# Chunk-select attention with a gated convolution: constants made on chip, bounds for fewer queries, gate sums over both halves

## The chip, the cores and the metric

The kernel runs on one core of a Trainium2 chip. The metric is the device time of one execution in microseconds, the median of several runs. Engines are named as in the profile: PE is TensorE, DVE VectorE, ACT ScalarE, POOL GpSimd, SP SyncE; PEld is TensorE's weight load.

## The reference

The input is q, k and v of 4 batches, 8 heads, 768 positions and 64 channels. Keys are cut into 24 chunks of 32. Each query sees the six chunks with the highest upper bound of its score, of those that are not in its future, and within them only positions up to its own. The attention output, with the heads side by side as 512 channels, goes through a gated unit: a causal convolution of five taps per channel gives the gate, a matrix gives the value, and a second matrix the output.

```python
ub = np.sum(np.maximum(q[:, :, :, None, :] * k_min[:, :, None, :, :],
                       q[:, :, :, None, :] * k_max[:, :, None, :, :]), axis=-1)
causal = pos[:, None] // chunk >= np.arange(nc)[None, :]
ub = np.where(causal, ub, -1000000000.0)
top_chunks = np.argsort(ub, axis=-1)[..., -top_k:]
scores = scale * np.matmul(q, k.transpose(0, 1, 3, 2))
mask = sel & (pos[:, None] >= pos[None, :])
attn = softmax of the masked scores
x = np.matmul(attn, v), heads side by side
gate_pre += conv_w[k][None, None, :] * xp[:, k:k + S, :]     # k = 0..4, xp padded in front
gate = 1.0 / (1.0 + np.exp(-gate_pre))
out = (gate * (x @ w_val)) @ w_out
```

A query below 192 has at most six chunks that are not in its future, so that all of them are among its six.

## The kernel before

Work goes by pairs of heads: 16 pairs, four to a batch. A pair's two heads fill 128 partitions. Every operation is recorded with an engine, a key and a cost (`Plan.add`); `Plan.order` then lists all operations by start times that it reckons from these costs, and picks among those that could start at nearly the same time the one with the smallest key. The table `SHIFT` moves the keys of groups of operations. The instructions are issued in that order, and every engine works its own off in order. PSUM's eight banks are given out by the same planner: `CAPS` says how many banks each kind of tile may hold (`w` is all that is not scores, value sums or spare). In places where TensorE would be idle, the planner puts dummy matmuls on `junk` into a spare bank (L530).

For each pair:

- `load` (L447) brings keys, queries and values, with two DMAs for each, one per head. Three buffers each.
- `kq`: TensorE transposes keys and queries (L548). ACT copies the keys out of PSUM to `k32` (L559), the queries to `q32` (L581), and their positive part to `rq` (L586). DVE takes the maximum and the minimum of each chunk (L565). GpSimd casts keys to `KE` (L573), queries to `QU` (L592) and values to `VA` (L636). `KE` also holds, in rows of its own, a -240 for each position's chunk, the E rows. From the extremes comes the table `KB` (L607, L614).
- `sel`/`part`: the bounds of a tile of 128 queries are two fp32 matmuls with `rq` and `q32` as weights and `KB` moving (L664), for the query tiles 1 to 5 (`SELT` is 5); tile 0 needs no selection. DVE adds a table of penalties for future chunks, `cfill`, into `t_mub` (L671), finds the eight highest (MAX8, L680), and compares with the sixth: `NS` is 1 where a chunk isn't chosen (L687). TensorE transposes `NS` (L697). For pairs 0 and 1 ACT and DVE copy the result straight into `QU`'s mask rows (L720). From pair 2 on (`MDMA = 2`) ACT copies it to `t_m` (L711), and two DMAs take it to `QU` (L715).
- `attn`: scores (L793) with `KE` as weights, into 11 banks of up to 512 columns; the E rows times the mask rows make the penalty. Exp on ACT (L800), the diagonal cut by GpSimd (L807), value sums (L824) with the exps as weights. A column of ones in `VA` gives the sum; DVE takes its reciprocal (L750) and multiplies (L754) into `t_onat`. A transposing DMA puts that into `xT` (L766); for the last pair TensorE and ACT do it (L775, L780).
- `moe_gate`: one channel tile per pair. The convolution runs over the two halves of 384 positions. The first `PTAPS` taps are matmuls with diagonal matrices, two for each tap since a weight is split into a high and a low part (L850); the other taps are added by DVE in PSUM (L859). `PTAPS` is 1, but 3 and 5 for the last two tiles of the last batch. ACT takes the tanh (L863).
- `moe_val` and `moe_out`, once a batch is complete: 32 value matmuls (L874), the product with the gate on DVE (L881), 24 output matmuls (L890), a copy (ACT L896, DVE L900) and a store (L903).

At the start, `constants` loads the identity, the E rows and `cfill` by DMA, fills other constants on DVE and GpSimd, and `warm` puts dummy matmuls (L507, L530) in front of TensorE's first transposes. `moe_diag` makes the 20 diagonal matrices on DVE (L931).

Of the kernel before, what the change touches and what calls it, by code (L numbers as in the profile page):

```python
# [9 lines left out]
FP = mybir.dt.float32  # L10
# [6 lines left out]
class Op:  # L17
    __slots__ = ("eng", "key", "cost", "fn", "kind", "reads", "writes", "new", "need", "ndep",
                 "outs", "after", "ready", "end", "num", "at")


class Plan:
# [18 lines left out]
    def add(self, eng, key, cost, fn, r=(), w=(), new=(), kind=None, at=0.0):  # L41
# [6 lines left out]
        key = round(key + self.shift.get(eng + ":" + what, 0.0), 4)  # L48
        o.eng, o.key, o.cost, o.fn, o.kind, o.new, o.at = eng, key, cost, fn, kind, new, at
        o.reads, o.writes = tuple(r), tuple(w)  # L50
# [33 lines left out]
    def order(self, bufs, caps, filler):  # L84
# [9 lines left out]
        for o in self.ops:  # L94
            tags.update(o.new)
            for x in set(o.reads + o.writes + tuple(n for n, _ in o.new)):
                users.setdefault(x, []).append(o)
        engs = ("PE", "ACT", "DVE", "POOL", "SP", "ACTQ")
        free = dict.fromkeys(engs, 0.0)
        wait = {e: [o for o in self.ops if o.eng == e and o.ndep == 0] for e in engs}  # L100
        last_pe = {n: [u for u in users[n] if u.eng == "PE"][-1] for n in tags
                   if tags[n] in caps and n in users}
# [14 lines left out]
        def clear(o, name):  # L117

            mine = set(users[name])
            for u in users[name]:  # L120
                for d in list(u.need) + [self.maker[x] for x in u.reads if x in self.maker]:
                    if d not in mine and d.end is None:
                        return False
                if u is not o and u.new and slot(u) is None:
                    return False
            return True

        def bank_of(tag):

            same, best = [], None  # L130
            for i, n in enumerate(banks):
                t = 0.0 if n is None else over(n)
                if n is not None and tags[n] == tag:
                    same.append(t)
                if t is not None and (best is None or t < best[0]):
                    best = (t, i)
            if best is None:
                return None
            lim = 0.0
            if len(same) >= caps[tag]:  # L140
                known = sorted(x for x in same if x is not None)
                k = len(same) - caps[tag]
                if len(known) <= k:
                    return None
                lim = known[k]
            return max(best[0], lim), best[1]

        def slot(o):
            t = 0.0
            for name, tag in o.new:  # L150
                if tag in caps:
                    got = bank_of(tag)
                    if got is None or tag == "w" and not clear(o, name):
                        return None
                    t = max(t, got[0])
                    continue
# [22 lines left out]
        def matmul(o, s):  # L179

            n = o.cost
            ld = max(pe["ldw"], pe["mm"])
            if o.kind == "u":
                m = max(s, ld + 0.043)
                ld = max(ld + 0.111, m)
                m = max(m + 0.043, ld + 0.043)
                pe["ldw"], free["PE"] = ld + 0.111, m + 0.043
            elif o.kind == "t":
                m = max(s, ld + 0.043)
                pe["ldw"], free["PE"] = ld + 0.108, m + n / 1200 + 0.001  # L190
            else:
                m = max(s, ld + 0.03)
                pe["ldw"], free["PE"] = ld + 0.028, m + n / 2400 + 0.002
            pe["mm"] = m
            if o.kind not in ("t", "x"):
                work.append((m, 0.13 if o.kind == "u" else n / 2400))
            pe["kind"] = "long" if o.kind is None and n >= 250 else o.kind
            o.end = m + (398 + n) / 2400 + 0.05
# [44 lines left out]
        while left:  # L243
# [6 lines left out]
            if e == "PE" and busy(s) < 0.42 and (s > free[e] + 0.12 or o.kind or o.cost < 250):  # L250
# [3 lines left out]
            for name, tag in o.new:  # L254
                if tag in caps:
                    i = bank_of(tag)[1]
# [7 lines left out]
                else:  # L264
# [31 lines left out]
def kernel(  # L296
# [10 lines left out]
    nc = tc.nc  # L307
# [17 lines left out]
    CC = (1, 0)  # L325
    SELT = NT - 1
    NBUF = 3

# [4 lines left out]
    MDMA = 2  # L333
    KBPOOL = True

    PTAPS = {(b, ct): 1 for b in range(B) for ct in range(NCT)}
    PTAPS[B - 1, NCT - 2] = 3
    PTAPS[B - 1, NCT - 1] = 5
    DTAPS = [max(PTAPS[b, ct] for b in range(B)) for ct in range(NCT)]

    ident_np = np.eye(128, dtype=np.float32)
    e_np = np.zeros((64, S), dtype=np.float16)
    for c in range(NCH):
        e_np[c, c * CH:(c + 1) * CH] = PEN
    cfill_np = np.zeros((128, SELT, 2, NCH), dtype=np.float32)
    for it in range(1, NT):
        for p in range(128):
            cfill_np[p, it - 1, :, (it * 128 + p) // CH + 1:] = -1.0e9
    cfill_np = cfill_np.reshape(128, SELT * 2 * NCH)

    ident_dr = nc.inline_tensor(ident_np, name="identc")
    e_dr = nc.inline_tensor(e_np, name="echunk")
    cfill_dr = nc.inline_tensor(cfill_np, name="cfill")
# [3 lines left out]
        "SP:kn": -0.2, "ACTQ:kn": -3.6, "SP:qn": 0.7, "ACTQ:E00": -0.6, "SP:vn": -0.62,  # L357
        "SP:cwn": -4.1, "DVE:KB": -1.2, "POOL:NS": 4.8, "POOL:VA": 1.2, "DVE:diag1": 3.8,
        "DVE:diag": 3.6, "PE:knT": -1.9, "ACT:k32": -2.0, "DVE:kmx": 1.8, "DVE:kmn": 1.6,
        "POOL:KE": -0.8, "DVE:KBh": 2.8, "PE:qnT": -1.88, "ACT:q32": -0.4, "ACT:rq": -0.2,  # L360
        "POOL:QU": -7.4, "DVE:top8": -2.0, "DVE:NS": -4.0, "PE:sT": -0.6, "POOL:kmrr": -1.2,
        "POOL:KBh": -4.6, "PE:s": 0.36, "bank0": 0.67, "ACT:P": 0.15, "POOL:Ptri": 0.3,
        "PE:av": -1.2, "bank1": 0.53, "DVE:rcp": -2.5, "DVE:onat": -1.8, "bank3": -0.2,
        "bank4": -0.06, "bank5": -0.04, "bank6": -0.55, "bank7": 0.1, "bank8": 0.12,
        "bank9": -0.62, "bank10": -0.24, "PE:pg": 1.23, "ACT:m16": -4.6, "PE:pv": 0.4,
        "DVE:gv": -3.4, "PE:po": 0.35, "ACT:osb": 1.5, "PE:xTp": 0.9,
    }
    CAPS = {"w": 5, "s": 4, "av": 2, "spare": 2}
    BUFS = {"kn": 3, "qn": 3, "vn": 3, "P5": 2, "kmx": 2, "kmr": 2,
            "q32": 2, "k32": 2, "rq": 2, "mub": 2, "top8": 2, "onat": 2, "rcp": 2, "osb": 4, "m16": 2}  # L370
# [13 lines left out]
    cfill = cpool.tile([128, SELT * 2 * NCH], FP, tag="cfill")  # L384
# [15 lines left out]
    PB = [ps.tile([128, 512], FP, tag=f"bank{i}", name=f"bank{i}") for i in range(Plan.NBANK)]  # L400
# [38 lines left out]
    def load(p, which, key, engs=("SP", "SP"), halves=((0, 1),)):  # L439
        b, h0 = p // NCT, 2 * (p % NCT)  # L440
        src = dict(kn=k, qn=q, vn=v)[which]
        for n, ws in enumerate(halves):
            t0, t1 = 3 * ws[0], 3 * ws[-1] + 3
            for hh in range(2):
# [12 lines left out]
    def constants():  # L457
        dve(-9, 0.2, lambda: nc.vector.memset(junk, 0.0), w=("junk",))
        sp(-9, 64, lambda: nc.scalar.dma_start(out=ident, in_=ident_dr.ap()), w=("ident",),
           eng="ACTQ")  # L460
        load(0, "kn", -8.9, ("SP", "ACTQ"), ((0,), (1,)))
        load(0, "qn", -8.88, ("SP", "ACTQ"), ((0,), (1,)))
        sp(-8.7, 96, lambda: nc.scalar.dma_start(out=KE[0][HP[1], 0, :], in_=e_dr.ap()),
           w=("E00",), eng="ACTQ")
        sp(-8.6, 120, lambda: nc.scalar.dma_start(out=cfill, in_=cfill_dr.ap()), w=("cfill",),
           eng="ACTQ")
# [3 lines left out]
        sp(-8.2, 10, lambda: nc.sync.dma_start(  # L470
            out=cwn, in_=moe_conv_w.rearrange("k (c p) -> (k c) p", p=128)), w=("cwn",))
        load(1, "vn", -8.1)
        for i in range(2):
            dve(-8.8, 0.15, lambda i=i: nc.vector.memset(KB[i], 0.0), w=(("KB", i),))
        for i in range(NBUF):
            dve(-8.7 + i, 0.5, lambda i=i: nc.vector.memset(QU[i][HP[1], 0, :], 0.0),
                w=(("QM", i, 0, 0), ("QM", i, 0, 1)))
            dve(-8.7 + i, 0.5, lambda i=i: nc.vector.memset(QU[i][HP[0], 1, :], 0.0),
                w=(("QM", i, 1, 0), ("QM", i, 1, 1)))
        dve(-8, 0.2, lambda: nc.vector.tensor_copy(out=identh, in_=ident), r=("ident",),  # L480
            w=("identh",))
        for i in range(NBUF):
            for hh in range(2):
                if i or hh:
                    pool(-4 + 1.5 * i, 0.87, lambda i=i, hh=hh: nc.gpsimd.tensor_copy(
                        out=KE[i][HP[1 - hh], hh, :], in_=KE[0][HP[1], 0, :]),
                        r=("E00",), w=(f"E{i}{hh}",))
        for i in range(2):
            pool(-7.5 + i, 0.6, lambda i=i: nc.gpsimd.memset(NS[i], 0.0),
# [4 lines left out]
        dve(-6, 0.1, lambda: nc.vector.memset(xT[:, :, 0:XP], 0.0),  # L494
# [3 lines left out]
    def warm():  # L498
        pe(-10, 512, lambda: spare("warm", 0, 512, True), r=("junk",), w=("warmed",),
           new=new("warm", "spare", [128, 512]))  # L500
        pe(-9.9, 6 * 512, warm_rows, r=("junk", "warm"), w=("warmed2",),
           new=new("warm2", "spare", [128, 512]))

    def warm_rows():

        def half(r, name, n, st=True):
            nc.tensor.matmul(out=T[name][:, 0:n], lhsT=junk[r, n % 128:n % 128 + 128],  # L507
                             rhs=junk[r, 0:n], start=st, stop=True, skip_group_check=True)

        lo, hi = slice(0, 64), slice(64, 128)  # L510
        for _ in range(4):
            half(lo, "warm", 512)
            half(hi, "warm2", 512)
        for _ in range(2):
            spare("warm", 0, 512, True)
        for _ in range(6):
            half(lo, "warm", 128)
            half(hi, "warm2", 128)
        for _ in range(3):
            spare("warm", 0, 128, True)  # L520
            half(lo, "warm", 128)
            half(hi, "warm2", 128)
        for _ in range(3):
# [488 lines left out]
```

## Time and profile before

| What | Value |
|---|---|
| Median of 3 runs | 201.23 us (200.47 to 202.47) |
| Profiled execution, its own time | 204.38 us |
| Its span, first to last instruction | 202.7 us |
| PE busy | 192.2 us (95%), 2140 matmuls |
| DVE busy | 167.8 us (83%) |
| ACT busy | 158.9 us (78%) |
| POOL busy | 127.8 us (63%) |
| DMA | 30.73 MB, mean 152 GB/s |

The page gives busy time per engine, and the span in 40 slices of about 5 us. Busy time is a union: two instructions that overlap count once, so that the mean duration of one is often more than the distance from one to the next. The chain of waits is followed back from the last instruction, and says at each step what released it. `PEclk` is the TensorE clock that was granted.

### The profile page before, as it was taken

To read this page: it belongs to the slowest core of one execution; us is meant where nothing else is said; L and a number is where in the kernel's file an instruction comes from. 1 tells how busy PE (TensorE), PEld (TensorE's weight loads), DVE (VectorE), ACT (ScalarE), POOL (GpSimd) and SP (SyncE) were. 2 spreads that over 40 slices of the span, in tenths; PEclk is the share of its full clock that TensorE was granted. 3 is DMA by queue.
4 is the path that set the end of the run, shared out by engine and by line. 5 is a ranking of instruction groups with operands and counts; after the bars stand their busy time and mean duration, and the time that the engine had idled before them with its cause. 6 is when DMAs were issued, how large, how long until landed. Compare 5 with 4: busy or idle time off the path is not lost.

```text
span 202.7 us, 6045 instructions
## 1 busy us (share of the span) xinstructions
PE 192.2 (95%) x2140; PEld 153.7 (76%) x2140; DVE 167.8 (83%) x518; ACT 158.9 (78%) x346; POOL 127.8 (63%) x282
## 2 busy tenths in 40 slices
PE   7998489999999999999999999999999999999992
PEld 1556469999986799979897899787989776665550
DVE  5059861977999899999998999999999999988251
ACT  0214368799899999899999999899998989995321
POOL 6647364898978979768867786589676872230000
PEclk9999757999999999999999999999999999999999
DMA  6999994799979699799889687223424112135044
GB/s 140 233 217 218 198 225 73 160 167 212 207 155 176 137 215 204 153 214 192 188 219 225 181 209 175 47 40 98 141 83 128 67 39 54 63 85 207 5 155 155
DMA packets 93277, 30.73 MB, mean 152 GB/s; under 512 B 88138, under 2 KB 90174, under 8 KB 93246
## 3 DMA queue, kind: packets, MB, share of 16 engines
q1 hardware_dynamic: 90222, 28.60, 64.7%
q0 software_dynamic: 1056, 1.05, 3.5%
q10 hardware_dynamic: 1968, 0.68, 1.5%
q8 instruction: 17, 0.28, 0.6%
q14 instruction: 14, 0.11, 0.2%
HBM read 21.27 MB, written 6.29 MB: 136 GB/s over the span
## 4 chain that ended last, share of the span: by engine, by line
PE 85%; ACT 7%; DVE 2%; DMA 2%; issue 1%; POOL 1%; ACTq 0%
PE bank L793 17%; PE bank L664 13%; PE bank L890 10%; PE bank L874 10%; PE bank L548 10%; PE bank L824 10%; PE bank L850 7%; PE bank L530 4%; ACT t_P L800 4%; PE bank L507 2%; PE bank L697 2%; DMA t_vn<-in_v_dram 2%; DVE diag L931 2%; ACT t_k L559 1%; POOL KE L573 1%
## 5 line engine op out<-in xcount | busy, mean ns | idle before, releaser
L800 ACT ACTIVATE t_P<-bank 128x512 f16<-128x512 f32 (+1 forms) x176 | 92.8, 614 | 2.1 <-PE bank L793 1.6
L859 DVE SCALAR_TENSOR_TENSOR bank<-xT,cwT,bank 128x384 f32<-128x384 f16 x116 | 70.9, 616 | 4.3 <-PE bank L850 3.4
L793 PE MATMUL bank<-QU,KE 128*128 128x128 f16 (+4 forms) x448 | 63.4, 252 | 1.3 <-ACT t_P L800 0.8
L592 POOL CAST QU<-t_q 64x384 f16<-64x384 f32 x64 | 32.0, 504 | 24.3 <-PE bank L793 15.6
L793 PEld LDWEIGHTS <-KE 88*128 88x128 f16 (+1 forms) x448 | 37.6, 107 | 8.0 <-issue 1.2
L807 POOL TENSOR_SCALAR_AFFINE_SELECT t_P<-t_P 128x384 f16<-128x384 f16 x64 | 32.9, 524 | 15.0 <-ACT t_P L800 13.2
L573 POOL CAST KE<-t_k 64x384 f16<-64x384 f32 x64 | 32.4, 514 | 8.7 <-ACT t_k L559 5.4
L824 PEld LDWEIGHTS <-t_P 128*128 128x128 f16 x672 | 29.9, 99 | 6.3 <-ACT t_P L800 2.3
L824 PE MATMUL bank<-VA,t_P 128*128 128x65 f16 x672 | 33.9, 193 | 0.4 <-ACT t_P L800 0.4
L664 PEld LDWEIGHTS bank<-KB,t_rq 128*128 128x128 f32 x160 | 27.5, 194 | 2.3 <-ACT t_q L581 0.9
L874 PE MATMUL bank<-xT,wval_sb 128*128 128x384 f16 x128 | 29.0, 326 | 0.0
L890 PE MATMUL bank<-wout_sb,t_gv 128*128 128x512 f16 x96 | 28.4, 379 | 0.0
L664 PE MATMUL bank<-KB,t_rq 128*128 128x48 f32 (+1 forms) x160 | 27.6, 254 | 0.5 <-ACT t_q L581 0.5
L664 PEld LDWEIGHTS bank<-KB,t_q 128*128 128x128 f32 x160 | 27.6, 193 | 0.4
L664 PE MATMUL bank<-KB,t_q 128*128 128x48 f32 (+1 forms) x160 | 27.0, 251 | 0.0
L565 DVE TENSOR_REDUCE t_kmr<-t_k 128x12 f32<-128x384 f32 x32 | 17.4, 545 | 7.7 <-ACT t_k L559 7.7
L559 ACT ACTIVATE t_k<-bank 128x384 f32<-128x384 f32 x32 | 16.5, 516 | 8.1 <-PE bank L548 7.7
L581 ACT ACTIVATE t_q<-bank 128x384 f32<-128x384 f32 x32 | 16.4, 516 | 7.9 <-PE bank L548 7.5
L850 PE MATMUL bank<-xT,diag 128*128 128x384 f16 x88 | 22.3, 326 | 0.0
L863 ACT ACTIVATE t_g<-bank 128x384 f32<-128x384 f32 x32 | 16.5, 518 | 5.0 <-DVE bank L859 2.9
L881 DVE SCALAR_TENSOR_TENSOR t_gv<-t_g,bank 128x384 f16<-128x384 f32 x32 | 17.6, 549 | 2.8 <-PE bank L874 2.4
L896 ACT ACTIVATE t_osb<-bank 128x512 f32<-128x512 f32 x22 | 13.0, 624 | 6.4 <-PE bank L890 5.4
(55 smaller groups left out, 277.6 us busy)
## 6 DMA issues: line engine op xcount, KB each, us to landing
t_vn<-in_v_dram SPq DMA_DIRECT2D x32, 192.0 KB
out_dram<-t_osb SPq DMA_DIRECT2D x24, 256.0 KB
t_kn<-in_k_dram SPq DMA_DIRECT2D x30, 192.0 KB
t_qn<-in_q_dram SPq DMA_DIRECT2D x30, 192.0 KB
QU<-t_m SPq DMA_DIRECT2D x28, 30.0 KB
wval_sb<-in_moe_w_val_dram POOLq DMA_DIRECT2D x1, 512.0 KB, 8.6
wout_sb<-in_moe_w_out_dram POOLq DMA_DIRECT2D x1, 512.0 KB, 7.9
xT<-t_onat SPq DMA_TRANSPOSE x15
```

The source lines that it names most:

```text
L548: lambda tl=tl: nc.tensor.transpose(out=T[name][:, tl * 128:(tl + 1) * 128], in_=T[which, p][:, 3 * w + tl, :], identity=ident),
L573: pool(k0 + (0.6 if p else 2.5), 0.56, lambda hh=hh: nc.gpsimd.tensor_copy(out=ke[HP[hh], hh, sl], in_=T["k32", p][HP[hh], sl]), r=(("k32" ...
L592: pool(k0 + 0.3, 0.56, lambda hh=hh: nc.gpsimd.tensor_copy(out=qu[HP[hh], hh, sl], in_=T["q32", p][HP[hh], sl]), r=(("q32", p, w), ("q32", ...
L664: pe(key, 48, lambda it=it, ts=ts, j=j, x=x: nc.tensor.matmul(out=cols(T[pu][:, it - 1 - i0, :]), lhsT=T[x, p][:, ts], rhs=cols(kb[:, j, : ...
L793: pe(kk, m, lambda hh=hh, c=c, jt=jt, q0=q0, m=m, bank=bank: nc.tensor.matmul(out=T[bank][:, c:c + m], lhsT=ke[KP[hh], hh, jt * 128:(jt + ...
L800: nc.scalar.activation(out=T[pt][:, 0:width], in_=T[bank][:, 0:width], func=AF.Exp, scale=0.125),
L807: nc.gpsimd.affine_select(out=ap, in_=ap, pattern=[[0, tris], [1, 128]], compare_op=ALU.is_ge, fill=0.0, base=0, channel_multiplier=-1)
L824: nc.tensor.matmul(out=T[pav][:, o0:o0 + D + 1], lhsT=T[pt][:, col:col + 128], rhs=va[:, hh, jt, :], start=st, stop=sp_, skip_group_check= ...
L850: nc.tensor.matmul(out=T[pg], lhsT=diag[ct][:, ki, hl, :], rhs=xT[:, slot, X0 + w * HB + ki:X0 + w * HB + ki + HB], start=(n == 0), stop=( ...
L859: dve(kk, 0.525, lambda pg=pg, i=i, c0=c0: nc.vector.scalar_tensor_tensor(out=T[pg], in0=xT[:, slot, c0:c0 + HB], scalar=cwT[:, i:i + 1], ...
L874: pe(key, HB, lambda ct=ct: nc.tensor.matmul(out=T[pv], lhsT=wval_sb[:, ct, et * 128:(et + 1) * 128], rhs=xT[:, slot0 + ct, XP + w * HB:XP ...
L890: pe(key, DM, lambda et=et: nc.tensor.matmul(out=T[po], lhsT=T["gv", b, et][:, s * 128:(s + 1) * 128], rhs=wout_sb[:, et, :], start=(et == ...
```

## The change

In `part`, bounds, comparison and mask now begin at query 192 (`SEL0`). Of tile 1 only the upper 64 queries are computed: their matmuls have 64 weights columns, and the transposed mask has 576 columns for 640. The penalty is added in PSUM, in place, and only for the four chunks of a tile's own 128 positions; MAX8 and the comparison read PSUM. The mask copies of all pairs go straight from PSUM to `QU` (`MDMA = 99`), one on DVE and one on ACT, and the 28 DMAs are gone.

In `moe_gate`, for the first three batches one DVE instruction adds a tap for both halves, over two banks, and one tanh takes both. All `PTAPS` are 1, so that in the last batch DVE adds four taps of each half where TensorE did up to five; 8 diagonal matrices are left of 20.

In `moe_val`, the last batch's value matmuls of the first three channel tiles have earlier keys, and hold a bank of a kind of their own (`v`, up to four) until the fourth.

In `constants`, the identity, the E rows and the penalties are made by GpSimd with fills and selects, the copies of the E rows and two fills move to DVE, and a dummy exp loads ACT's table. Pair 0's keys are loaded first; its casts to `KE` and `QU` are made by ACT from PSUM. `warm` keeps eight short dummies, one per bank, and one of 512 columns; the planner adds five more ahead of the first transposes. Loads are made three pairs ahead. There is one spare bank for two. The planner now gives out several banks at once, reckons with half the clock before 7 us, has other limits for dummies, and every number in `SHIFT` is another.

Some branches of the new code are not taken (`SHUF = 99`, `KDIR`, `RQP`, `UTAPS` all 0).

The core of the diff:

```diff
+    SEL0 = 192
-    MDMA = 2
+    MDMA = 99
     PTAPS = {(b, ct): 1 for b in range(B) for ct in range(NCT)}
-    PTAPS[B - 1, NCT - 2] = 3
-    PTAPS[B - 1, NCT - 1] = 5
+    WIDE = {(b, ct) for b in range(B - 1) for ct in range(NCT)}
-    CAPS = {"w": 5, "s": 4, "av": 2, "spare": 2}
+    CAPS = {"w": 5, "s": 4, "av": 2, "spare": 1, "v": 4}
...
+        def identity():
+            nc.gpsimd.memset(ident, 0.0)
+            select(ident, [[-1, 128]], ALU.not_equal, 1.0, 0, 1)
+
+        def chunk_rows():
+            t = KE[0][HP[1], 0, :]
+            nc.gpsimd.memset(t, PEN)
+            select(t, [[1, S]], ALU.is_ge, 0.0, 0, -CH)
+            select(t, [[-1, S]], ALU.is_ge, 0.0, CH - 1, CH)
...
             for hh in range(2):
+                if p == 0:
+                    act(k0 + 0.3, 0.4, lambda hh=hh: nc.scalar.copy(
+                        out=ke[HP[hh], hh, sl], in_=T[name][HP[hh], :]),
+                        r=rd, w=(("KE", iN, hh, w),))
+                    continue
...
         for it in its:
-            ts = slice(it * 128, (it + 1) * 128)
+            ts = slice((it + 1) * 128 - rows(it), (it + 1) * 128)
             for j, x in enumerate(("rq", "q32")):
-                    out=cols(T[pu][:, it - 1 - i0, :]), lhsT=T[x, p][:, ts],
+                    out=cols(bound(it - 1 - i0))[0:rows(it)], lhsT=T[x, p][:, ts],
...
-            out=cols(T["mub", p][:, i0:i1]), in0=cols(T[pu]), in1=cols(cf[:, i0:i1]),
-            op=ALU.add),
+            out=own(), in0=own(), in1=cfill[:, i0:i1], op=ALU.add),
...
-                    in_=T["mub", p][:, it - 1, s * NCH:s * NCH + m]),
+                    in_=bound(it - 1 - i0)[:, s * NCH:s * NCH + m]),
...
+            for ki in range(max(taps, 1), late):
+                dve(kk, 0.525 if not whole else 0.93, lambda i=i, ki=ki, w=w:
+                    nc.vector.scalar_tensor_tensor(
+                        out=both() if whole else T[pgs[w]], in0=x_of(X0 + ki, w),
+                        scalar=cwT[:, i:i + 1], in1=both() if whole else T[pgs[w]],
+                        op0=ALU.mult, op1=ALU.add),
...
-            pe(key, HB, lambda ct=ct: nc.tensor.matmul(
+            pe(key if early is None or ct == NCT - 1 else early, HB,
+               lambda ct=ct: nc.tensor.matmul(
...
-        if p + 2 < NPAIR:
-            for which in ("kn", "qn", "vn"):
-                load(p + 2, which, p - 0.5)
+        if p + 3 < NPAIR:
+            for n, which in enumerate(("kn", "qn", "vn")):
+                load(p + 3, which, p + 0.1 * n, ENGS)
```

## The prediction

> **What bounds the kernel now.** I read the page first (busy shares, the 40 slices, the chain of waits), then a table of three stages cut at the times at which the slices change, then the chain in order of time, then the start and the tail instruction by instruction.
>
> ```profile
> PE   7998489999999999999999999999999999999992
> DVE  5059861977999899999998999999999999988251
> PEclk9999757999999999999999999999999999999999
> PE 85%; ACT 7%; DVE 2%; DMA 2%; issue 1%; POOL 1%; ACTq 0%
> ...
> core 0: us, PE busy (x) PEld busy (x) DVE busy (x) ACT busy (x) POOL busy (x), PEclk, DMA share, GB/s
> 0.00:40.00 40.00, 34.63 (x267) 24.34 (x268) 23.73 (x90) 17.10 (x37) 24.09 (x53) 0.87 1.02 186
> 40.00:167.00 127.00, 125.94 (x1600) 110.25 (x1600) 120.82 (x383) 120.43 (x266) 99.59 (x222) 1.00 0.72 155
> 167.00:203.00 36.00, 31.66 (x278) 19.11 (x275) 23.30 (x47) 21.41 (x44) 4.14 (x8) 1.00 0.30 102
> ```
>
> The chain is TensorE for 85%. A busy PE isn't a full one, so I priced its work by the pieces of the chain: L664 (bounds) x10 1.05 us, that is 0.108 each; L548 x6 0.66; L824 x23 0.71; L850 x6 0.98; L874 x6 0.97; L890 x12 2.59; the scores L793 of one pair are 5376 columns, 2.3 us at the pace of the others. Times their counts: bounds 34.6, transposes L548 21.3, scores 36, value sums L824 20.8, gates L850 14.3, L874 20.7, L890 20.7, mask transposes L697 4.4: 172.7 us of real work. In the first 40 us only some 15 us of it is done (49 of 192 transposes, 48 of 320 bounds, 28 scores, 42 value sums). The other 158 us fill the 159 us from 40 to the last matmul at 198.8. So from 40 us on TensorE is the bound and full, with DVE and ACT at 95% beside it, and the first 40 us lose 25 us. Two things can pay: an earlier start, and less TensorE work.
>
> The start, from the timeline and the chain:
>
> ```profile
> 5.10 1.28 ACT L559 ACT_TABLE_LOAD   x1 [5.10 <-DMA t_kn<-in_k_dram]
> 7.57 2.98 PE L530 MATMUL bank<-junk 128*128 128x512 f16 x13
> 10.39 0.38 PE L548 MATMUL bank<-ident,t_kn 128*128 128x128 f32 x2
> ...
> 18.73 3.16 DVE diag L931 x11
> ...
> 23.50 0.40 PE L697 MATMUL bank<-identh,NS 128*128 128x128 f16 x2 [2.59 <-DVE NS L687]
> 26.36 1.09 ACT L800 ACTIVATE t_P<-bank 128x512 f16<-128x512 f32 x2 [1.13 <-PE bank L793]
> ```
>
> The keys have been there since 5 to 6 us (what waited for them went on at 5.10), but the first transposes stand behind a fixed run of dummy matmuls until 10.4. Then DVE makes 20 diagonals, 11 of them on the chain ahead of the selection; TensorE runs dry at 21 to 23.5, and its clock is halved in three slices. The first exp is at 26.4, the masks of pair 1 at 40.06.
>
> [...] here the clock fell to 0.50 at 23 us after two idle microseconds or so, and back at 33. [...] 384 elements took 548 ns from PSUM (L754) and 545 from SBUF (L565). [...]
>
> **The change, part by part.**
>
> Start. Constants come from GpSimd, the SP and ACT queues issue keys of pair 0, keys of pair 1, queries of pair 0 first, and the first transposes stand behind 8 + 6 dummies. *Identity*: on GpSimd it stands behind a 64x768 fill (0.75, from NS 128x640 at 0.65), two selects of that size (1.0 each, from 0.52 for 384), and small ones (1.1): 0.8 + 3.9 gives 4.7, [...]. The dummies end at about 4.6 and cost nothing. *Key transposes*: 5.5 to 6.7. *ACT*: seven copies at its pace of 0.39, 6.2 to 9; then eight for the queries (the loads before them are about 1.2 MB at some 215 GB/s, there by 8), 12.1, three more key copies, 13.3. *DVE*: its memsets and five E copies end at about 8; minima and maxima follow the second key copy at 8.5, five at 0.46, then the bound table (1.3 in the trace, and 0.3): 12. *Selection*: bounds 0.8, DVE 0.9, transposes and mask copies 0.9, scores 0.5: first exp at 15.5, against 26.4. The diagonals, now 8 instead of 20, stand behind it. Gain 11 us. Bounds: [...] if TensorE also stays warm at 12 to 20, where it was cold at 23 to 33, up to 15. After that the plan does the same work up to the masks of pair 1, ACT about 0.4 per copy, so I carry the 11 us on unchanged.
>
> Bounds and mask transposes. The tile of queries 128 to 255 is computed for 64 queries: 32 of 160 bound matmuls, two records each, 0.054 saved per record by the halved load: 3.45 us. 16 of 80 mask transposes move 64 columns instead of 128: 0.027 each, 0.4. All of this is on the bound engine: -3.85. If the load weren't shortened, 0 instead of 3.45.
>
> DVE in the middle, per pair, at the pace of back-to-back instructions. Gate adds: eight at 0.585 (3.50 us for six in the tail) become four of 768 elements; [...] 0.985 each: 4.7 to 3.9. Penalty and its tile: 0.33 to 0.2. Mask copy: new, 0.40 to 0.45 (24x640 took 489, 24x384 355). MAX8 from PSUM: ten, [...] I take 0.02, since L754 against L565 shows nothing. DVE per pair 10.3 to 10.1, against 10.4 for TensorE after the change. So DVE stays just under the bound; [...]. ACT: mask copy 0.61 for 0.71, Relu of 192 for 256 columns (-0.04), tanh of 768 for two of 384 (about -0.2): -0.3 a pair. In the start it takes over eight casts of GpSimd (3.1 us, in the walk above).
>
> Mask DMAs. 28 issues go from SP (1.6 us a pair); the path PSUM to SBUF to QU becomes one copy. TensorE waited 0.5 us in all for them: 0. The DVE mask copy waits for five transposes and has 1 to 15 other instructions between it and the comparison that feeds them, in all but one place two or more: 0 to 0.3 a pair, hidden by TensorE.
>
> Loads three pairs ahead: TensorE never waited on a load after the start, so 0. One spare bank less, and 41 dummies instead of 109: they filled gaps, so 0.
>
> Tail. The last batch stays at 384 and loses TensorE taps: 24 gate matmuls of 0.163, 3.9 us, go from TensorE and 12 adds of 0.585, 7.0 us, come to DVE. Behind the last mask transpose (at 167.0 now, 35.7 before the end) the order as built leaves TensorE 30.1 us (45 scores, 84 value sums, 16 gates, 64 value matmuls, 48 out) and DVE 32 adds, 16 gate products, 4 normalisations, 2 outputs and the mask: 18.7 + 7.8 + 2.4 + 1.3 + 0.4 = 30.6. After either comes the last output, 0.6, and its store: the span ends 3.3 us after the last copy. So 34 to 35.1 instead of 35.7: -1, not -3.9. If DVE also has a backlog there, +2; if TensorE decides, -2.
>
> Sum: -11 - 3.85 - 1 = -15.9 us on a span of 202.7: 186.8; the profiled execution would go from 204.38 (1.7 outside the span) to 188.5. The median of the runs is 201.23, 3.15 under the profiled one; I carry the difference over: 185.3 us.
>
> **Rivals.**
> (A) *DVE takes over in the middle.* For: it is at 95% already, ten MAX8 move to PSUM. Against: the two paces above. [...]
> (B) *The start comes only a little earlier*: the identity is the last but one thing that GpSimd makes, [...] or the queues stall on keys of pair 1, whose transposes stand ahead of the queries of pair 0, and TensorE goes cold again. Gain 5 instead of 11: about 191.
> (C) *Slower: PSUM banks.* A wide gate holds two banks for 4 x 0.985 + 0.84 = 4.8 us (one for 2.9 now), and the bounds keep theirs until the comparison, some 2 to 6 us with adds between the MAX8, instead of 0.4. TensorE is in order: a matmul without a bank stops all. From 1.0 us of such waiting per pair (16 pairs, 16 us) the gain is gone; at 1.3 us it is 206. Against: TensorE now waits 0.3 us on L859 in the whole run, and of the shared banks five are still allowed to these tiles.
> (D) *It doesn't do what it says*: the shorter tile saves no load time and the start is as B: 195.
>
> **How the numbers follow.** Forecast 0.58, A 0.14, B 0.13, D 0.03, C 0.12. The forecast's own range is 179 (start -15, tail -2, the rest as summed, and 1 us from ACT) to 190; A, B and D reach to 196. Range 179 to 196; what is left out is C and the extremes of the others, 2 in 10. A measurement tells about 1%, 2 us, from no change. Faster is all but C: 0.88; of C's 0.12, 0.03 fall within 1% and 0.09 are slower.
>
> **What would show it.** Right: first exp at 13.5 to 18 us, first key transposes near 5.5; bound weight loads of two sizes, the smaller at half; wide adds near 1.0 us and MAX8 near its 0.16; TensorE without a gap from some 28 us on; the last 10 us led by DVE L988 instead of L850. Wrong: transposes that wait on GpSimd after 8 us; half clock between 10 and 25 us for more than 5 us; DVE at 99% with TensorE waiting on it between 40 and 150 us; TensorE or its loads waiting on a bank for more than 0.5 us a pair.

## The result: 262.1 us, 30% slower, and the profile after

The median of four executions is 262.12 us (262.05 to 265.2), that of the kernel before, run beside it, 201.85. The ratio is 1.305, 95% interval 1.291 to 1.320. The profiled execution has a span of 260.4 us. The prediction was 185.3 us (179 to 196). Ratios here and below leave out the slower executions of a kernel (e17: 198.5 to 200.1 us at a granted clock of 0.97 to 0.98, against 193.5 to 194.7 at 0.99 to 1.00); medians are over all executions.

The page after, first the rows by slices (6.5 us each), then the chain of waits by engine:

```profile
PE   6889888588578887684888866966966899999993
DVE  7787946348457778756378534565655387999992
PEclk9999999759959999999599955699897599999999
...
PE 57%; DVE 20%; ACT 11%; issue 5%; DMA 3%; POOL 2%; ACTq 0%; DVEq 0%; POOLq 0%
```

And the table of three stages of the same run, with the columns of the prediction's table:

```profile
0.00:42.00 42.00, 35.99 (x381) 29.14 (x382) 30.81 (x125) 33.63 (x78) 28.49 (x70) 1.00 1.17 203
42.00:210.00 168.00, 127.22 (x1221) 100.50 (x1220) 100.71 (x269) 97.71 (x201) 81.56 (x181) 0.84 0.46 93
210.00:260.40 50.40, 45.75 (x451) 29.25 (x449) 43.15 (x100) 33.62 (x67) 12.05 (x26) 1.00 0.32 107
```

In the middle no engine is the bound: TensorE is busy for 127 of 168 us, DVE and ACT for about 60% of it, where before all three stood at about 95% or more. The granted clock is 0.84 in this stage, below 0.6 in six of the slices. Of TensorE's 51.4 idle us 40.8 lie between the start of the first wide gate add, at 44.1 us, and 210 us; from there on it is nearly full, 45.75 of 50.40 us.

The start, from the timeline:

```profile
4.31 0.29 POOL L495 TENSOR_SCALAR_AFFINE_SELECT ident<-ident 128x128 f32<-128x128 f32 x1
4.66 0.88 PE L572 MATMUL banks<-ident,t_kn 128*128 128x128 f32 x6 [0.43 <-POOL ident L495]
...
14.65 0.83 PE L876 MATMUL banks<-QU,KE 128*128 128x128 f16 x10
15.24 0.59 ACT L883 ACTIVATE t_P<-banks 128x512 f16<-128x512 f32 x1
```

The identity is ready at 4.6 us, the first transposes start at 4.66, and the first exp at 15.24 instead of 26.36: the start did what was predicted. The middle lost all of it and much more. In the new kernel L741 are the bounds, L876 the scores, L883 the exps, L988 the gate adds and L1023 the output matmuls. Who waits, in the whole run (us in total, times, longest):

```profile
ACT t_P L883 <- DVE banks L988: 16.4, 13, 1.8
PE banks L876 <- DVE banks L988: 13.2, 14, 1.7
DVE banks L988 <- ACT t_P L883: 7.9, 9, 1.3
...
DVE banks L988 <- PE banks L876: 5.9, 9, 1.4
```

The gate adds (L988) wait for exps (L883) and scores (L876), and these for gate adds. By their data they have nothing to do with each other: scores and gates are in different banks. A shortage of banks could make a score wait for a gate, but hardly the second, third or fourth add of a gate, whose banks are long its own, for an exp, a bound or an output matmul. Yet so it is. Of one gate (banks 1 and 7), the second to fourth add on DVE's timeline (start, duration, what, and in brackets the idle time before and what ended it):

```profile
150.11 1.02 DVE L988 SCALAR_TENSOR_TENSOR banks<-xT,cwT,banks 128x768 f32<-128x768 f16 x1 [1.33 <-PE banks L741]
153.31 1.02 DVE L988 SCALAR_TENSOR_TENSOR banks<-xT,cwT,banks 128x768 f32<-128x768 f16 x1 [2.17 <-PE banks L1023]
...
156.78 1.02 DVE L988 SCALAR_TENSOR_TENSOR banks<-xT,cwT,banks 128x768 f32<-128x768 f16 x1 [2.20 <-PE banks L741]
```

And the first two of another (banks 0 and 1):

```profile
210.56 1.02 DVE L988 SCALAR_TENSOR_TENSOR banks<-xT,cwT,banks 128x768 f32<-128x768 f16 x1
...
211.62 1.02 DVE L988 SCALAR_TENSOR_TENSOR banks<-xT,cwT,banks 128x768 f32<-128x768 f16 x1
```

What differs is where the planner put the gate's two banks. The change makes all eight banks one tile, `PALL`, and the wide access is `PALL[:, i:j + 1:j - i, 0:HB]`: banks i and j, with a stride over those between. From the start of a gate's first add to the end of its fourth, the twelve wide gates took:

| Banks between i and j | Gates (i, j) | Four adds, us |
|---|---|---|
| 0 | (0,1) (6,7) | 4.2, 4.2 |
| 1 | (1,3) and three times (2,4) | 5.9, 6.6, 6.3, 7.1 |
| 3 | (2,6) (3,7) | 8.4, 8.3 |
| 5 or 6 | (0,6) (0,7) (1,7) (1,7) | 9.1, 9.5, 10.0, 9.7 |

The semaphores that the built program's instructions wait for say the same (each is named for the engine or the DMA that raises it). The second and third add of the first gate, banks 0 and 6, and the first two of the last, banks 6 and 7:

```
L988 TensorScalarPtr 128x2x384 [waits DVE, PE, Activation]
L988 TensorScalarPtr 128x2x384 [waits DVE, PE, Activation]
...
L988 TensorScalarPtr 128x2x384 [waits DMA, PE]
L988 TensorScalarPtr 128x2x384 [waits DVE]
```

In the two gates on neighbouring banks none of the six later adds waits for TensorE or ACT; in the ten others 25 of 30 do.

**Theory 1**: the layer that sets the semaphores puts a wide access in order with everything that touches a bank from i to j, those between included: a false order. **Theory 2**: the prediction's rival C, too few banks, as a wide gate holds two. **Theory 3**: the wide instruction itself, or DVE's load. **Theory 4**: the lost clock is the cause, not a consequence.

### The profile page after: what moved, and what is told of

It is laid out like the page before. It is cut to its first block, busy times and chain, and to the rows that moved or that the text cites. A ratio compares the mean times of both kernels' runs of the same rounds, so it can differ in the third digit from the quotient of the medians.

```text
span 260.4 us, 5793 instructions
## 1 busy us (share of the span) xinstructions
PE 209.0 (80%) x2048; PEld 158.9 (61%) x2048; DVE 174.7 (67%) x492; ACT 165.0 (63%) x343; POOL 122.1 (47%) x275
## 3 DMA queue, kind: packets, MB, share of 16 engines
q0 software_dynamic: 1056, 1.05, 2.8%
## 4 chain that ended last, share of the span: by engine, by line
PE 57%; DVE 20%; ACT 11%; issue 5%; DMA 3%; POOL 2%; ACTq 0%; DVEq 0%; POOLq 0%
DVE banks L988 16%; PE banks L876 12%; PE banks L741 10%; PE banks L907 8%; PE banks L1007 7%; PE banks L1023 7%; PE banks L572 6%; ACT t_P L883 5%; ACT t_g L993 3%; PE banks L964 3%; PE banks L780 2%; DMA t_qn<-in_q_dram 2%; DMA t_kn<-in_k_dram 1%; POOL t_P L890 1%; ACT t_k L587 1%
## 5 line engine op out<-in xcount | busy, mean ns | idle before, releaser
L883 ACT ACTIVATE t_P<-banks 128x512 f16<-128x512 f32 (+1 forms) x176 | 93.5, 586 | 34.2 <-PE banks L876 16.5
L988 DVE SCALAR_TENSOR_TENSOR banks<-xT,cwT,banks 128x768 f32<-128x768 f16 (+1 forms) x80 | 67.7, 861 | 29.6 <-ACT t_P L883 7.9
L876 PE MATMUL banks<-QU,KE 128*128 128x128 f16 (+4 forms) x448 | 68.3, 259 | 19.1 <-DVE banks L988 13.2
L876 PEld LDWEIGHTS <-KE 128*128 128x128 f16 (+1 forms) x448 | 40.5, 111 | 19.9 <-issue 12.0
L1007 PE MATMUL banks<-xT,wval_sb 128*128 128x384 f16 x128 | 33.8, 352 | 5.2 <-DVE banks L988 4.2
L907 PE MATMUL banks<-VA,t_P 128*128 128x65 f16 x672 | 31.1, 205 | 8.3 <-DVE banks L988 6.2
L741 PEld LDWEIGHTS banks<-KB,t_rq 128*128 128x128 f32 (+1 forms) x160 | 27.9, 204 | 15.1 <-issue 5.8
L741 PEld LDWEIGHTS banks<-KB,t_q 128*128 128x128 f32 (+1 forms) x160 | 28.2, 204 | 7.0 <-issue 3.9
L741 PE MATMUL banks<-KB,t_rq 128*128 128x48 f32 (+3 forms) x160 | 30.4, 275 | 2.4 <-ACT t_g L993 0.9
L741 PE MATMUL banks<-KB,t_q 128*128 128x48 f32 (+3 forms) x160 | 29.2, 267 | 2.2 <-DVE banks L988 2.2
L1023 PE MATMUL banks<-wout_sb,t_gv 128*128 128x512 f16 x96 | 27.3, 391 | 2.4 <-DVE banks L988 2.0
L1014 DVE SCALAR_TENSOR_TENSOR t_gv<-t_g,banks 128x384 f16<-128x384 f32 x32 | 17.1, 550 | 10.8 <-PE banks L1007 10.7
```

Source lines behind the costliest of these rows:

```text
L741: pe(key, rows(it), lambda it=it, ts=ts, j=j, x=x: nc.tensor.matmul(out=cols(bound(it - 1 - i0))[0:rows(it)], lhsT=T[x, p][:, ts], rhs=col ...
L876: pe(kk, m, lambda hh=hh, c=c, jt=jt, q0=q0, m=m, bank=bank: nc.tensor.matmul(out=T[bank][:, c:c + m], lhsT=ke[KP[hh], hh, jt * 128:(jt + ...
L883: nc.scalar.activation(out=T[pt][:, 0:width], in_=T[bank][:, 0:width], func=AF.Exp, scale=0.125),
L907: nc.tensor.matmul(out=T[pav][:, o0:o0 + D + 1], lhsT=T[pt][:, col:col + 128], rhs=va[:, hh, jt, :], start=st, stop=sp_, skip_group_check= ...
L988: nc.vector.scalar_tensor_tensor(out=both() if whole else T[pgs[w]], in0=x_of(X0 + ki, w), scalar=cwT[:, i:i + 1], in1=both() if whole els ...
L1007: lambda ct=ct: nc.tensor.matmul(out=T[pv], lhsT=wval_sb[:, ct, et * 128:(et + 1) * 128], rhs=xT[:, slot0 + ct, XP + w * HB:XP + (w + 1) * ...
```

## Experiments on the middle

**Other bank numbers, same order.** The numbers of a plan's banks are arbitrary. A permutation after planning leaves every instruction, the order, the holding times and the number of banks as they are:

```diff
     order = plan.order(BUFS, CAPS, filler)
+    PERM = (3, 1, 5, 0, 6, 7, 4, 2)
+    for x in plan.place:
+        plan.place[x] = PERM[plan.place[x]]
...
```

(what is left out swaps the banks of a gate's two halves where the lower one would come second). This is e1; in e2 `PERM` is (5, 0, 6, 4, 2, 3, 1, 7). The twelve gates have 31 banks between their pairs in the changed kernel, 3 in the first permutation, 43 in the second.

> Same instructions, same planned order, only the numbers of the eight banks are exchanged, so that the two banks of a wide gate lie side by side (9 of 12 gates) or with one between them (3). Theory 1, false order: a wide access is kept apart from everything in the banks that lie between its two; the 12 gates of the changed kernel have 31 such banks between them, and cost some 75 us over 187, 2.4 us each; with 3 left 187 + 7 = 194 us (188 to 202), TensorE full in nearly all slices. Theory 2, too few banks (the prediction's C): exchanging numbers changes nothing, 262. Theory 3, the 1.02 us instruction itself or DVE as the bound: 262. Theory 4, the lost clock: it goes where the idle time goes, so 262 unless 1 holds.

> The same exchange the other way: the two banks of every wide gate as far from each other as the plan allows, 43 banks between the pairs instead of 31, and no gate with neighbours. Theory 1: slower than the changed kernel, 262 + 12 x 2.4 = 291 us if it goes by banks, 262 + 2 x 7.5 = 277 if it goes by gates; 272 to 295. Theories 2 and 3: 262, within 1%.

e1 took 211.84 us (207.98, the profiled execution, to 212.7), e2 285.07 (ratio to before 1.402, 1.391 to 1.413). The time goes with the banks between, with nothing else changed: taking e1's 207.98, the 28 banks from 3 to 31 cost 54 us, the 12 from 31 to 43 cost 23, 1.9 us a bank both times. But e1 lies above the 188 to 202 us that were expected, so something besides the false order costs time too. The TensorE row of e1, then of e2:

```profile
PE   6897989999889999999999994999975778999991
```

```profile
PE   6889895985769887677869758878668595799994
```

e1 is nearly full until the slice at 124 us. The three gates that still have a bank between start at 123.2, 149.6 and 163.0 us, in the slices with gaps. This refutes theories 2 and 3 as the main cause.

**Halves in place of wide instructions.** The plan stays, and with it the places and the two banks per gate:

```diff
-                dve(kk, ..., lambda i=i, ki=ki, w=w: nc.vector.scalar_tensor_tensor(out=both() ...
+                dve(kk, ..., lambda ...: [nc.vector.scalar_tensor_tensor(out=T[pgs[x]],
+                    in0=half_of(X0 + ki, x), ..., in1=T[pgs[x]], ...) for x in ws]
```

and the tanh alike.

> Planned order, banks and holding times stay; at each place of a wide add or tanh stand two instructions for 384 elements, each on one bank. Theory 1: no access spans banks, so no false order; DVE has 8 x 0.62 instead of 4 x 1.02 us per gate, 0.9 more on 12 gates, partly hidden: 190 us (186 to 198). Theory 2: two banks are still held for a gate and a little longer, 262 or more. Theory 3 by length: two instructions take longer than one, so 262 or more; by DVE's load the same.

198.67 us (198.4 to 200.01); ratio 0.979 (0.973 to 0.986). TensorE's row and clock:

```profile
PE   6897998999698899999999999999999999999991
...
PEclk9999999999999999999999999999999999999999
```

Some 63 us are gone, though the plan gives each gate its two banks for as long as before, and neither TensorE nor an exp waits for a gate add any more. The clock came back as the idle time went (1.000 in the mean, for 0.894 in the changed kernel): theory 4 isn't needed, though no run here holds the clock and keeps the waits. But 198.7 is not the 190 that was expected, nor the 185.3 of the prediction: something else costs some 10 us.

**Neighbours by the planner**, which then makes a new order:

```diff
+            if n == 2:
+                two = [(max(at[i], at[i + 1]), i) for i in at if i + 1 in at]
```

> The wide instructions stay; the planner may give a wide gate only two neighbouring banks, and makes a new order for that (its own reckoned end goes from 182.9 to 187.3 us). Theory 1: no bank between, 189 us (184 to 195), TensorE full from 45 to 245 us. Theory 2: a tighter choice of banks, so slower than 262. Theory 3: 262.

202.91 us (ratio 1.003, 0.999 to 1.006). Theory 1 is met as far as some 60 us go, but the result misses the expected 184 to 195 and is 4 us over the halves. The planner's own reckoned end had grown by 4.4 us (182.9 to 187.3); that the new order is the reason isn't shown by a run of its own. The cheap way is the permutation, with the three gates that it doesn't reach split into halves:

> The bank numbers of the first exchange, and the three gates whose banks still have one between them are split into halves; nine gates keep the wide add and tanh. No access has a bank between. Theory 1: like the halves (198.7) less what a wide add saves on DVE: four at 1.05 for eight at 0.57, 0.33 us on each of nine gates, 3 us where DVE decides: 196 us (194 to 199). If neighbouring banks too are kept apart by the wide access: above 205.

198.21 us (ratio 0.983, 0.974 to 0.993). e5 and e1 differ in these three gates alone: 198.2 against 208.0 us in the profiled executions. And, in the kernel before, the single tile by itself:

```diff
-    PB = [ps.tile([128, 512], FP, tag=f"bank{i}", name=f"bank{i}") for i in range(Plan.NBANK)]
+    PALL = ps.tile([128, Plan.NBANK, 512], FP, tag="banks", name="banks")
+    PB = [PALL[:, i, :] for i in range(Plan.NBANK)]
```

> The kernel before, with its eight banks as parts of one tile instead of eight tiles, and nothing else. Theory 1: no access spans two banks, so no change, 203 (201 to 205). A rival of theory 1, that the single tile itself orders accesses of different banks: 215 or more.

202.89 us (ratio 0.997, 0.993 to 1.002): no change. The single tile does no harm without an access that spans banks.

## Experiments on what was left

**Is DVE a second bound?** In e3's order, the last tap of the twelve gates is left out:

```diff
-                    ... for x in ws]
+                    ... for x in ws if len(ws) < 2 or ki < 4]
```

> The halves version in its order, but the last of the four taps that DVE adds is left out in the twelve gates of the first three batches: 24 adds of 0.57 us less, 13.6 us of DVE, 1.1 per pair; TensorE does the same work. If DVE shares the bound from 40 us on, so that TensorE cannot run at its full pace there (rival A of the prediction): 198.7 falls by 4 to 10, to 189 to 195. If TensorE or the loads are the bound: 197 to 199.

201.07 us (197.87 to 205.25; ratio 0.985, 0.972 to 0.997, against e3's 0.979): nothing gained with 24 adds of 0.57 us, 13.6 us, less for DVE to do (its busy time is 162.9 us for 173.9). In this order DVE isn't the bound, against rival A.

**Is the shortened weight load worth 3.45 us?** In e3's order, the narrow bounds load 128 columns again:

```diff
             ts = slice((it + 1) * 128 - rows(it), (it + 1) * 128)
+            if it == 1:
+                ts = slice(192, 320)
...
-                    out=cols(bound(it - 1 - i0))[0:rows(it)], lhsT=T[x, p][:, ts],
+                    out=cols(bound(it - 1 - i0)), lhsT=T[x, p][:, ts],
```

> The halves version in its order, but the bound matmuls of the tile with 64 queries load 128 columns of weights again (queries 192 to 319; the upper half of the result isn't used): 64 more half loads, 3.45 us more of TensorE. If TensorE is the bound all through, as the prediction had it: 198.7 + 3.4 = 202. If DVE shares the bound in the middle: +0 to +1.5, 199 to 200.

196.85 us (196.04 to 197.39; ratio 0.975, 0.969 to 0.981): not the 3.4 us more that were expected, if anything a little faster than e3's 0.979. A possible reason is the change itself, from weights of 128 columns to 64 and back; the expectations below call this the switch theory. The traces measure what such a change costs, not what TensorE does in that time. The same piece of the plan, first with the narrow tiles (e16 below), then with tiles of 128 (e13 below), start and duration:

```profile
107.91 0.38 PE L1033 MATMUL banks<-wout_sb,t_gv 128*128 128x512 f16 x1
108.22 0.53 PE L780 MATMUL banks<-identh,NS 64*128 64x64 f16 x5
108.59 0.59 PE L1033 MATMUL banks<-wout_sb,t_gv 128*128 128x512 f16 x2
109.12 0.32 PE L741 MATMUL banks<-KB,t_rq 128*64 128x48 f32 x2
109.36 0.39 PE L1033 MATMUL banks<-wout_sb,t_gv 128*128 128x512 f16 x1
109.68 0.32 PE L741 MATMUL banks<-KB,t_q 128*64 128x48 f32 x2
109.93 0.34 PE L975 MATMUL banks<-xT,diag 128*128 128x384 f16 x1
110.10 0.32 PE L741 MATMUL banks<-KB,t_rq 128*128 128x48 f32 x2
```

```profile
106.23 0.38 PE L1035 MATMUL banks<-wout_sb,t_gv 128*128 128x512 f16 x1
106.45 0.44 PE L782 MATMUL banks<-identh,NS 128*128 128x128 f16 x5
106.73 0.59 PE L1035 MATMUL banks<-wout_sb,t_gv 128*128 128x512 f16 x2
107.16 0.32 PE L743 MATMUL banks<-KB,t_rq 128*128 128x48 f32 x2
107.31 0.38 PE L1035 MATMUL banks<-wout_sb,t_gv 128*128 128x512 f16 x1
```

Read the distances of the starts, not the durations, which are alike. From 108.59 to 109.36 there are two output matmuls (0.216 each, from the prediction's 2.59 us for 12) and one narrow bound (two records): 0.77 - 0.43 = 0.34 us. With 128 columns it is 0.58 - 0.43 = 0.15. The transposes with a 64-wide first one take 108.59 - 107.91 - 0.216 = 0.46 us, with 128 only 0.28. So a narrow bound costs 0.19 more and a narrow transpose 0.18, an estimate of 32 x 0.19 + 16 x 0.18 = 9 us on TensorE. Other places agree for the bounds: in e16, from 40 us on, the 25 full ones that stand alone between long matmuls have a median of 0.16 us, the 4 narrow ones 0.36.

The weight loads of e16 show where the difference arises:

```profile
109.68 0.19 PEld L741 LDWEIGHTS banks<-KB,t_q 128*64 128x64 f32 x2 [0.23 <-issue]
109.93 0.10 PEld L975 LDWEIGHTS <-diag 128*128 128x128 f16 x1
109.93 0.36 PEld L741 LDWEIGHTS banks<-KB,t_rq 128*128 128x128 f32 x2
```

The two narrow loads are shorter, 0.19 us against 0.36. But they start at 109.68 together with their own matmul, as does the first full load behind them, at 109.93, while the load of the next full bound starts at 109.93 too, 0.17 ahead of its matmul at 110.10 and under another one. In these lines no load is hidden where the width changes.

Three runs test this, and one with DVE relieved besides. The transposes become:

```diff
-                out=T[pt][:, c0:c0 + m], in_=ns[0:m, i0 + i, :], identity=identh[0:m, 0:m]),
+                out=T[pt][:, c0:c0 + 128], in_=ns[:, i0 + i, :], identity=identh),
```

and the bounds load 128 columns as in e7.

> The halves version in its order, with 128 columns and 128 rows of weights everywhere: the bounds of the tile with 64 queries load 128 columns (as in the run with 128-column loads), and its mask transpose moves 128 rows and columns (the surplus is overwritten by the next). Switch theory: [...] in the traces such a bound costs 0.35 us with its surroundings where a full one costs 0.155, 0.19 x 32 = 6 us, and the transposes 0.18 x 16 = 3 us. TensorE has 9 us less to do than in the halves version (198.7); as DVE is at 97% beside it from 60 us on, only a part shows: 192 to 196. Prediction's step (the shorter tile saves 3.45 + 0.4): slower than 198.7, 200 to 202.

> The version with nine wide gates on neighbouring banks and three in halves (198.2), with weight tiles of 128 everywhere as in the run beside this. Switch theory, with DVE as the second bound: wide adds take 3 us from DVE, so that 2 to 3 us more show than with halves: 190 to 194. If DVE doesn't share the bound: as the run beside this, within 1 us.

> The run with weight tiles of 128 everywhere, and in the twelve gates of the first three batches the last of the four taps that DVE adds is left out (13.6 us of DVE). With the narrow tiles this did nothing (201). Two bounds side by side: now that TensorE has 9 us less, DVE decides more, and 3 to 6 us go: 187 to 191. If DVE doesn't matter: as without the omission, 192 to 196.

e9: 197.05 us (ratio 0.962, 0.956 to 0.969). e10: 195.52 (0.954, 0.946 to 0.961). e11: 196.54 (0.955, 0.947 to 0.963), so DVE again decides little, against the 3 to 6 us that were expected; e9 and e10 lie 1.0 and 1.5 us over their expected ranges. From e3's 0.979 to e9's 0.962 the tiles of 128 bring 1.7%, 3.5 us of the 9; why the rest doesn't show is open. The other direction, one edit in the kernel before:

```diff
-                pe(key, 48, lambda it=it, ts=ts, j=j, x=x: nc.tensor.matmul(
-                    out=cols(T[pu][:, it - 1 - i0, :]), lhsT=T[x, p][:, ts],
+                m = 64 if it == 1 else 128
+                pe(key, 48, lambda it=it, ts=slice(ts.stop - m, ts.stop), m=m, j=j, x=x: nc.tensor.matmul(
+                    out=cols(T[pu][:, it - 1 - i0, :])[0:m], lhsT=T[x, p][:, ts],
```

> The kernel before; only the bounds of query tile 1 load 64 columns of weights (queries 192 to 255) and write 64 rows; the selection of that tile is then not the reference's. Nothing else is changed. Prediction's step: 64 half loads save 0.054 each on a full TensorE, 3.45 us: 199.8. Switch theory: 32 matmuls at +0.19 us, 6 us where TensorE is full (28 of 32): +4 to +6, 207 to 209.

207.07 us, ratio 1.016 (1.010 to 1.023): the narrow bounds alone cost the kernel before 1.6%, 3.3 us, where the prediction had them save 3.45.

**Are the loads a bound?** The first transposing DMA took 9.3 us in e9, from its issue at 32.91 to the gate matmul that waited for it, while the weight matrices came in. In e10's kernel they are issued later (e13), the loads from pair 3 on are left out (e14), or both (e15):

```diff
+    for what, behind in ((("wvald",), ("xT", 2, 0)), (("woutd",), ("xT", 3, 0))):
+        o = next(o for o in order if o.writes == what)
+        order.remove(o)
+        n = next(n for n, u in enumerate(order) if u.eng == "SP" and behind in u.writes)
+        order.insert(n + 1, o)
```

> The best version so far (0.954 of the kernel before) in its order, only GpSimd's DMAs of the two weight matrices are issued later, behind the transposing DMAs of pairs 2 and 3 (about 57 and 66 us instead of 33 and 39). DMA theory: the first transposing DMA, 9.2 us to the waiting gate matmul, falls to 4 or 5, and 2 to 4 us of that reach the end: ratio 0.935 to 0.945, 191 to 193. If the loads alone fill the queues: no change, 0.954. If the order or the compute engines are the limit: no change.

> The best version so far in its order, but the loads of keys, queries and values of pairs 3 to 15 are left out; these pairs work on the data of the first three. DMA theory: the transposing DMA takes 2 to 3 us, 40 to 80 us runs at full pace, and 5 to 8 us go: ratio 0.915 to 0.93, 187 to 190. If the order or the compute engines limit: 0.95 or more.

> Both: loads of pairs 3 to 15 left out and the weight matrices later. DMA theory: like the run with few loads or 1 us less, 186 to 190. If weights and loads each did half, the two gains add up; if neither moved the time, this doesn't either.

192.09 (191.9 to 193.62), 191.9 and 192.13 us; ratios 0.955 (0.949 to 0.961), 0.954 and 0.955. The three are alike, and their ratios are e10's: without nearly all loads the kernel is no faster, so the loads don't bound. The expected gain from the DMAs (0.915 to 0.945) didn't come, though TensorE's wait for the transposing DMA, 2.3 us in e9, is gone in all three. e13's order once more with the narrow tiles, and e10's kernel once more:

> The version of 192.1 us (nine wide gates on neighbouring banks, weight matrices later) in its order, with the narrow weight tiles of the change again: bounds that load 64 columns, mask transposes of 64 rows. Switch theory: 32 x 0.19 + 16 x 0.18 = 9 us more of TensorE, two thirds of which show: 198 (196 to 200). Prediction's step: 192.1 - 3.85 = 188.2.

> The version with nine wide gates on neighbouring banks and weight tiles of 128, weight matrices still loaded at 33 and 39 us; this is the kernel of the run with 195.5 us once more, now beside the others. If the moved weights matter: 194 to 196, TensorE does 33 us of work between 40 and 80 us. If the difference was the chip's: 191.5 to 192.5, the same as with the weights moved.

e17: 198.52 (193.45 to 200.09; ratio 0.959, 0.949 to 0.969). Its ratio doesn't differ from e13's, and e13 ran on another chip, so no gain from moving the weights is shown. e16, the narrow tiles again: 196.36 (ratio 0.971, 0.966 to 0.976), 4.3 us over e13 between medians and some 3 by the ratios, again on another chip, where the prediction's step gives 3.85 less.

No version is shown to be faster than e13: 192.09 us, against 262.12 for the change as made. Its page:

```profile
PE   6897997999998999999999999999999999999991
...
PE 68%; DVE 11%; POOL 7%; DMA 4%; ACT 4%; issue 3%; ACTq 0%; POOLq 0%; DVEq 0%
```

## Why the prediction was wrong, step by step

**The step that failed: the wide gate add's waits, put at nothing, 63 us.** The part "DVE in the middle" priced the wide add as an instruction ("four of 768 elements", 0.985 each, its estimate; measured 1.022 alone, 1.06 from start to start, and 0.620 alone for 384 elements) and nowhere asked what it would have to wait for. It waited for what worked in the banks between its two, and that work waited for it: 262.1 us with the wide accesses, 198.7 with halves. It was to be read in the diff, `PALL` and its strided access, and in the waits of the built program.

**Rival C had the sign and not the mechanism.** It gave "slower" 0.09 and named TensorE waiting on banks, and such rows appeared. But e3 plans two banks per gate just as long and TensorE doesn't wait for the adds, and e1 and e2 differ from the change in bank numbers only. That the sign of C came true is luck: a wait "on a bank" doesn't say whether the bank is scarce.

**Start, -11: right.** First exp at 15.24 (15.5 predicted). With the prediction's prices per matmul, an estimate, TensorE had 15 us of work behind it at 40 us before, 25 after, 27 in e13. Rival B falls: the first key transposes start at 4.66 us (5.5 predicted), and the first exp is 11.1 us earlier, not 5.

**Bounds and mask transposes, -3.85: wrong sign.** The step that failed here is "0.054 saved per record by the halved load". The 0.108 that it halves was taken from ten bounds in a row (1.05 us, which is 0.105 each). Most bounds stand between long matmuls, and there one takes 0.15 us for its two records, in the kernel before too: the bound at 104.19 in that kernel has output matmuls at 103.97 and 104.34 around it, and 0.37 - 0.216 is 0.15. Its two weight loads take 0.41 us, but start at 103.97, beside the output matmul in front. So little of the load is left to shorten. The price of 0.108 also made the bounds too large a part of TensorE's 172.7 us, so that the 158 us that seemed to fill the 159 were too many. On top of that comes the change of tile width, 0.19 us for each narrow bound in e16. On the kernel before the bounds are +3.3, and with the transposes it is +4.3 between e13 and e16.

**DVE in the middle: right in size, and hidden.** MAX8 has means of 161 to 175 ns by shape from PSUM and 154 to 168 from SBUF, under 0.01 us more (0.02 was taken). Taking 13.6 us from DVE gained nothing that shows, in e6 and in e11; for these orders rival A falls.

**Tail, -1: right in sign, half the size.** The last mask transpose starts at 225.2, 35.2 us before the end, where it was 35.7 before. The prediction's sums give 30.1 or 30.6 + 0.6 + 3.3, 34.0 to 34.5 us; the 35.1 that it gives as the other end isn't worked out.

**Loads, 0: not refuted.** e14 gains nothing over e13 or, by ratio, over e10.

**Profiled execution to median, -3.15: wrong.** I carried over that the profiled execution of before was 3.15 us over its median. But that median was one of three runs: with more of them the kernel before has medians of 201.85 to 204.0. After, the profiled execution and the median are both 262.1.

The sum without the false order, with the bounds at 0 and without the carried 3.15, is 188.5 + 3.85 = 192.35 us. e13, which has the rest of the change and neither fault, took 192.06 in its profiled execution. That this comes so close is partly luck: the sum starts from one execution at 204.38, and against the 202.89 beside it e13 saves 10.8 us between medians and some 9 by the ratio, where start and tail were to bring 12. The terms aren't proved one by one, but no large one is missing.

## What to carry to other kernels

When an access becomes one instruction over several buffers, ask what the layer that sets the semaphores takes it to touch: here a stride over other buffers tied it to those between, 1.9 us for each bank. It shows as waits between instructions that share no data, and permuting the buffers' numbers tests it without changing anything else. Price a matmul by the distance of starts where it really stands, between its neighbours, and try one size of weight tile in a stream: the smaller tile saved nothing here and cost 0.19 us each time.

## What the runs showed of the hardware

- A bound (two records) with 64 columns of weights between ones of 128 cost 0.34 us where a full one cost 0.15. Its loads, and the first one behind it, started with their own matmuls and not ahead of them (e16, 109.68 and 109.93). Weights of 88 rows among those of 128 showed no such gap: in e16 a score of 88 rows and 384 columns at 112.03 takes 0.16 us to the next start, as a gate matmul of 128 rows and 384 columns at 110.26 does.
- MAX8 of eight elements took 162 ns from PSUM in the changed kernel, 158 from SBUF in the kernel before.
- GpSimd's first select in the changed kernel started at 1.61 us, 0.07 behind the end of the fill before it.
- 13.6 us of adds taken from DVE saved nothing in e3's order (ratio 0.985 in e6 against 0.979 in e3).
